# The first block's preparation in an attention and SwiGLU block: work moved from GpSimd to VectorE, loads and memsets reordered

## Chip, cores and metric

The kernel runs on one core of a Trainium2 chip. The metric is device time in microseconds (us); less is better. Engines: TensorE (PE in the profile; PEld is its weight load) multiplies, VectorE (DVE), ScalarE (ACT) and GpSimd (POOL) work on tiles, SyncE (SP) issues the transfers (DMAs) of one queue. Each engine works through its own instructions in the order in which the program gives them.

## The reference

A transformer block over x of 2048 positions by 512 features, all in float32: a modulation of six rows from the vector c, a layer norm with scale and shift, attention of 32 heads of 16 features over a sliding window of 256 positions, and a SwiGLU of 1792 features.

```python
mod = (silu(c) @ w_mod).reshape(1, 6, 1, 512)      # sa, ca, ga, sb, cb, gb
h = layernorm(x) * (1 + ca) + sa
x = x + ga * attention(h, wqkv, wo)                # causal, window 256, 32 heads
h = layernorm(x) * (1 + cb) + sb
x = x + gb * ((silu(h @ w1) * (h @ w3)) @ w2)
```

## The kernel before

The positions are cut into four blocks of 512 (`NB`), a block into four tiles of 128. A product in nearly full float32 is made of three products of float32r parts: a matrix is split into its rounded form (part 0) and the remainder (part 1), and part 0 by part 0, part 0 by part 1 and part 1 by part 0 are added up. So whatever TensorE multiplies has first to be cast and then subtracted.

The change lies in the opening, the first 100 us or so. There the order of all work is written out by hand: each step is handed to `at` with a time (in units of its own, none of the chip's), and all steps are recorded sorted by these times. What a step waits for follows from the data and from the buffers; the times only set each engine's order. The dictionary `W` and the dictionary `Y` hold them. `h0` is -40, the time of the first block.

What the opening does, with the names used below:

- `load_x` loads a tile of x into `xt` (six buffers, `XB`); `load_mod` loads four 256 KB pieces of w_mod into `stage`, `load_wv` (n=0) the four pieces of the values' weights into the same memory, `load_wqk` (n=0) a group's query and key weights into `wqr`. SyncE's queue issues all but c and the first modulation's pieces, which ScalarE's queue issues.
- `modulation(j, s)`: TensorE multiplies silu(c) with row block j of w_mod (`row`, L570 of the profile), ScalarE copies the result (`out`, L575), TensorE turns it into columns (`turn`, L583) and VectorE stores them in `modc` (L592). For j=2 and 5 it is instead spread by a product (L580), copied (L589) and stored to memory (`g_dr`, L590). The order of j is 0, 1, then 3, 4, 2, 5 among the values' products; the rows of 3 and 5 are the third and the sixth.
- `ln1(b)`: VectorE takes the statistics of four tiles (L335, L336), GpSimd the reciprocal root (L330), VectorE normalises (L340), TensorE transposes (L628) a feature group k of 128, ScalarE scales and shifts it (`h`, L347), VectorE makes part 0 (cast, L349) and part 1 (subtraction, L350) in `hT`.
- `load_wv` with n=1 makes part 0 of the values' weights for group k on ScalarE (`wvh`, L606), with n=2 part 1 on GpSimd (`wvl`, L608). `load_wqk` does the same for queries and keys: part 0 on ScalarE (L418), part 1 on GpSimd (L421).
- `values(t)`: twelve products (L650), three for each k, and a copy by ScalarE (L654). `unit_a(u)`: twelve products (`pj`, L433) for a head group and a block, three copies on ScalarE, two subtractions on GpSimd (`mix`, L451), and six transfers (`rows`, L456), two for each of three parts (qk0, qk1, qk2), into `ring`, the tile of keys and queries. `unit_b(u)`: the score products over `ring` (L486), which need all six, and their row maxima on VectorE (L493).
- `ring_fill(b)` writes the constant rows of `ring` for a block: five memsets of 1024 elements. For b=0 two are VectorE's, the rest GpSimd's.
- Three small tiles are made on VectorE behind the first block's statistics: `odd` (L305), `identr` (L398), the masks `later` and `mskr` (L393, L395). The masks are cut from `mskw`, which lies in the buffer of `wqr`, so the first load of wqk waits for them, and SyncE's queue behind it.

Each transfer counts up one of eight semaphores, in turn, and waits for the transfer eight before it.

Of the kernel before, what the change touches and what calls it, by code (L numbers as in the profile page):

```python
# [18 lines left out]
P = 128  # L19
KC = D // P  # L20
NT = S // P
NB = 4
BT = S // NB
# [13 lines left out]
         o=(9.93, 10.63), job=(-0.855, 2.493, 10.058))  # L37
# [6 lines left out]
W = dict(m=0.15, s=0.1, a=0.32, t=0.541, p=0.377, vs=1.762, vo=0.422, wq=-2.02, ws=-0.376, wv0=-1.811, wv=0.3, wvk=0.474, h0=0.539, h=6, hb=6.874, ls=3.287, la=1.146, rf=7.313, v=2, vt=1.75, m0=1.5, mt=0.7, ml=0.241, A=1.268, At=7.876, B=9.889)  # L44
MXB = 3
STB = 3
MODL = 'CECECECE'
NL = 3
XB = 6
PTB = 9  # L50
NU = NQ * NB
NP = NF // 2
# [236 lines left out]
def block_kernel(ctx: ExitStack, tc: tile.TileContext, x, wqk, wv, wo, w13, w2, c, wmod, out):  # L289
    nc = tc.nc  # L290
# [4 lines left out]
    ident = cst.tile([P, P], F32, name="ident")  # L295
# [4 lines left out]
    nc.gpsimd.memset(o32, 1.0 / 32)  # L300
    odd = cst.tile([P, 1], F32, name="odd")

    for hh in range(2):
        r = slice(64 * hh, 64 * hh + 64)
        nc.vector.tensor_reduce(  # L305
            out=odd[r], in_=ident[r].rearrange("p (c o) -> p c o", o=4)[:, :, 2 - 2 * hh:4 - 2 * hh],
            op=ALU.add, axis=mybir.AxisListType.XY)
    modc = cst.tile([P, 4, KC], F32, name="modc")
    sc32 = cst.tile([P, KC, 32], F32, name="sc32")

# [57 lines left out]
    ring = ap.tile([P, 3, 2, S], F32R, name="ring")  # L368
# [24 lines left out]
    nc.vector.tensor_scalar(later, mskk[:, 0], 0.0, None, op0=ALU.is_lt)  # L393
    mskr = ap.tile([P, 2, P], F32R, name="mskr")
    nc.vector.tensor_copy(mskr, mskk)  # L395
    mskk = mskr.bitcast(F32)
    identr = ap.tile([P, P], F32R, name="identr")
    nc.vector.tensor_copy(identr, ident)  # L398

    def ring_fill(b):  # L400
        for hh in range(2):
            k = ring.bitcast(F32)[:, 2 - 2 * hh, :, b * BT:(b + 1) * BT]
            eng = nc.vector if b == 0 and hh == 0 else nc.gpsimd
            eng.memset(k[:NM] if hh == 0 else k[:NS], 0.0)
            if hh:
                eng.memset(k[NS:NM], 1.0)
            eng.memset(k[NS:NS + 2], 1.0 - hh)

    WQ = {}

    def load_wqk(g, n):
        if n == 0:
            raw = a1.tile([P, KC, P], F32, name="wqr", bufs=1)
            nc.sync.dma_start(raw, wqk[g])
            WQ[g] = [None, None, raw]
        elif n == 1:
            WQ[g][0] = a1.tile([P, KC, P], F32R, name=f"wq0{g % 2}", bufs=1)
            nc.scalar.activation(WQ[g][0], WQ[g][2], AF.Copy)  # L418
        else:
            WQ[g][1] = a1.tile([P, KC, P], F32R, name=f"wq1{g % 2}", bufs=1)  # L420
            nc.gpsimd.tensor_tensor(out=WQ[g][1], in0=WQ[g][2], in1=WQ[g][0].bitcast(F32),  # L421
                                    op=ALU.subtract)

    def unit_a(u, t0, at, y=X):

# [130 lines left out]
    nc.vector.tensor_copy(sc32, sc[:, :, None].to_broadcast([P, KC, 32]))  # L556

    def modulation(j, s, t0, at):

        v = {}  # L560

        def bank(n):
            v[n] = psA.tile([P, BT], F32, name="mx", bufs=MXB)
            return v[n]

        def row():

            ps = bank(0)
            for k in range(KC):
                nc.tensor.matmul(ps[32 * k:32 * k + 32, :], sc32[:, k], stage[:, s, k], start=True,  # L570
                                 stop=True)

        def out():
            v["e"] = p0.tile([P, D], F32, name="h32", bufs=3)
            nc.scalar.activation(v["e"], v[0], AF.Copy)  # L575

        def turn():
            ps = bank(1)
            if j in (2, 5):
                nc.tensor.matmul(ps[:32], o32[:, :32], v["e"], start=True, stop=True)  # L580
                return
            for n in range(KC):
                nc.tensor.matmul(ps[:, n:n + 1], v["e"][:, n * P:(n + 1) * P], o32[:, 0:1],  # L583
                                 start=True, stop=True)

        def end():
            if j in (2, 5):
                r = p0.tile([P, D], F32, name="h32", bufs=3)
                nc.scalar.activation(r[:1], v[1][:1], AF.Copy)  # L589
                nc.sync.dma_start(g_dr[j // 5:j // 5 + 1, :], r[:1, :])  # L590
            else:
                nc.vector.tensor_scalar_add(modc[:, (0, 1, 0, 2, 3)[j]], v[1][:, :KC],  # L592
                                            float(j in (1, 4)))

        for n, fn in enumerate((row, out, turn, end)):
            at(t0 + W["m"] * n, fn)

# [3 lines left out]
    def load_wv(k, n):  # L601
        raw = stage[:, 0, k]
        if n == 0:
            nc.sync.dma_start(raw, wv[:, k])
        elif n == 1:
            nc.scalar.activation(wvh[:, k], raw, AF.Copy)  # L606
        else:
            nc.gpsimd.tensor_tensor(out=wvl[:, k], in0=raw, in1=wvh.bitcast(F32)[:, k],  # L608
                                    op=ALU.subtract)

    def ln1(b, ts, ta, th, at):
        v = {}
# [20 lines left out]
        for i in range(4):  # L633
            at(ts + W["s"] * i, lambda i=i: stats(i))
            at(ta + W["a"] * i, lambda i=i: apply(i))
            at(th + W["t"] * i, lambda i=i: turn(i))
            at(th + W["t"] * i + W["p"], lambda i=i: parts(i))
            if b + 1 < NB:
                at(th + (W["t"] * 3 + 0.1 if i > 1 else -0.5), lambda i=i: load_x(4 * b + 4 + i))
        at(ts + W["s"] * 3 + 0.1, rstd)  # L640

    def values(t, t0, at):
# [947 lines left out]
```

## Time and profile before

| | us |
|---|---|
| time, median of 3 runs (lowest to highest) | 989.64 (989.48 to 990.66) |
| profiled execution: its time | 987.77 |
| profiled execution: span of the page | 986.0 |
| third modulation's row on TensorE starts | 29.77 |
| sixth modulation's row on TensorE starts | 45.10 |
| first score product starts | 50.66 |

The last three come from the timeline of the profiled execution, counted from the span's start. Rows of a timeline give start and duration in us, the engine, the line, the operation, what it writes and reads, a count, and in brackets the idle time before it with what ended it. An engine's name with a q is its queue: there an instruction that only waits or issues.

### The profile page before, as it was taken

Reading aid. Unit: us, or ns where it says so; the run is one execution under the profiler, and the core shown is the slowest. Engines: PE = TensorE matmul, PEld = TensorE weight load, DVE = VectorE, ACT = ScalarE, POOL = GpSimd, SP = SyncE. Lnnn points to the kernel's source line nnn. Section 1 sums busy time; section 2 is a strip of 40 time slices with the busy share of each in tenths; the row PEclk is TensorE's granted clock in tenths of the full one; section 3 lists DMA queues with packets and bytes.
Section 4 is the critical chain, followed back from the end, with each engine's and each line's share of the span. In section 5 each row is a group of like instructions: output and inputs, shape, how many; then the busy total and the mean of one; then the engine's idle time right before and its main releaser. Section 6 shows DMA issues by size and latency. Waiting matters only on the chain.

```text
span 986.0 us, 17173 instructions
## 1 busy us (share of the span) xinstructions
PE 944.6 (96%) x5316; PEld 717.4 (73%) x5316; DVE 717.9 (73%) x1999; ACT 554.2 (56%) x1252; POOL 609.8 (62%) x775
## 2 busy tenths in 40 slices
PE   5999999999999999997888999999999999999998
PEld 2578777777777776764566778878888888888886
DVE  7775889899989999996467676755568655555455
ACT  3433887787878787874577864333445344433330
POOL 7441787787868686864476588897737555443420
PEclk9999999999999999997999999999999999999999
DMA  8621354444544444435891558765336423312102
GB/s 280 189 87 34 125 187 142 142 141 142 177 150 148 145 150 143 142 131 152 218 268 68 175 169 285 235 206 192 121 96 208 147 73 96 96 59 81 38 22 85
DMA packets 80671, 141.64 MB, mean 144 GB/s; under 512 B 9538, under 2 KB 22338, under 8 KB 80580
## 3 DMA queue, kind: packets, MB, share of 16 engines
q1 hardware_dynamic: 79860, 139.50, 43.8%
q10 hardware_dynamic: 720, 1.05, 0.3%
q8 instruction: 42, 0.69, 0.3%
q14 instruction: 49, 0.40, 0.1%
HBM read 85.72 MB, written 34.61 MB: 122 GB/s over the span
## 4 chain that ended last, share of the span: by engine, by line
PE 74%; POOL 8%; DVE 7%; DMA 6%; issue 2%; ACT 2%; SPq 1%; POOLq 0%; DVEq 0%; ACTq 0%
PE mx L1361 11%; PE st L1361 11%; PE mx L486 8%; PE pj L433 7%; PE st L736 7%; PE st L1454 6%; PE po L712 6%; PE mx L1454 6%; PE pj L1361 4%; PE st L650 3%; PE pj L1454 2%; POOL w L953 2%; POOL pt L764 2%; POOL qk L451 1%; DMA ring<-qk 1%
## 5 line engine op out<-in xcount | busy, mean ns | idle before, releaser
L493 DVE CUSTOM_DVE_ANT_0 junk<-mx,mskq 128x384 bf16<-128x384 f32 (+2 forms) x512 | 256.5, 527 | 35.4 <-PE mx L486 34.1
L953 POOL TENSOR_TENSOR w<-w,w 128x512 fp32r<-128x512 f32 (+2 forms) x56 | 107.7, 1936 | 124.4 <-ACT w L952 93.4
L486 PE MATMUL mx<-ring 96*128 96x384 f32 (+2 forms) x512 | 155.9, 342 | 9.9 <-DMA ring<-qk 6.9
L736 PE MATMUL st<-ring 100*128 100x384 f32 (+2 forms) x512 | 156.3, 346 | 2.8 <-ACT pt L748 1.4
L764 POOL TENSOR_SCALAR_AFFINE_SELECT pt<-pt 128x256 f32<-128x256 f32 x268 | 108.6, 408 | 73.4 <-ACT pt L757 63.1
L433 PE MATMUL pj<-hT,wq 128*128 128x512 f32 x384 | 136.3, 405 | 1.5 <-DVE hT L350 1.2
L486 PEld LDWEIGHTS mx<-ring 96*128 96x128 f32 x512 | 94.1, 190 | 43.5 <-DVE mt L493 25.0
L757 ACT ACTIVATE pt<-st 128x256 f32<-128x256 f32 x268 | 96.1, 386 | 41.9 <-DVE st L754 34.4
L736 PEld LDWEIGHTS st<-ring 100*128 100x128 f32 x512 | 95.8, 190 | 24.8 <-issue 8.0
L712 PE MATMUL po<-pt,vS 128*17 128x384 f32 (+2 forms) x1408 | 96.6, 391 | 1.4 <-POOL pt L764 0.9
L451 POOL TENSOR_TENSOR qk<-qkr,qk 128x512 fp32r<-128x512 f32 x64 | 82.7, 1292 | 15.9 <-ACT qkr L439 15.6
L754 DVE COPY_PREDICATED st<-later,st 128x128 f32<-128x128 uint8 x268 | 72.1, 291 | 10.2 <-PE st L736 6.3
L433 PEld LDWEIGHTS pj<-hT,wq 128*128 128x128 f32 x384 | 71.7, 190 | 8.7 <-DVE hT L350 1.5
L1432 ACT ACTIVATE wq<-g 128x512 fp32r<-128x512 f32 x28 | 17.7, 633 | 91.0 <-PE st L1454 31.6
L712 PEld LDWEIGHTS po<-pt,vS 128*17 128x17 f32 x1408 | 33.2, 97 | 47.2 <-issue 21.3
L1392 DVE TENSOR_TENSOR t<-mx,t 128x512 f32<-128x512 f32 x50 | 34.4, 688 | 45.4 <-PE mx L1361 31.0
L1361 PE MATMUL st<-b,w 128*128 128x512 f32 x258 | 64.6, 392 | 0.8 <-DVE b L1258 0.4
L1361 PE MATMUL mx<-b,w 128*128 128x512 f32 x252 | 62.7, 394 | 1.1 <-ACT mx L976 1.1
L748 ACT ACTIVATE pt<-st 128x384 f32<-128x384 f32 (+2 forms) x128 | 52.7, 434 | 17.5 <-DVE st L744 13.9
L1392 DVE TENSOR_TENSOR t<-st,t 128x512 f32<-128x512 f32 x47 | 32.3, 687 | 41.5 <-PE st L1361 23.8
L781 POOL TENSOR_SCALAR_AFFINE_SELECT sm<-sm 128x256 f32<-128x256 f32 x109 | 41.9, 407 | 28.1 <-ACT sm L771 24.1
L1361 PEld LDWEIGHTS st<-b,w 128*128 128x128 f32 x258 | 48.1, 188 | 11.9 <-DVE b L1258 0.8
(265 smaller groups left out, 2088.8 us busy)
## 6 DMA issues: line engine op xcount, KB each, us to landing
ring<-qk SPq DMA_DIRECT2D x192, 128.0 KB
o_dr<-os SPq DMA_DIRECT2D x32, 256.0 KB
w<-wsum SPq DMA_DIRECT2D x14, 512.0 KB
w<-w2g SPq DMA_DIRECT2D x14, 512.0 KB
jb<-in_w SPq DMA_DIRECT2D x24, 256.0 KB
wraw<-in_w SPq DMA_DIRECT2D x7, 768.0 KB
w<-wraw SPq DMA_DIRECT2D x14, 384.0 KB
vS<-in_wmod SPq DMA_DIRECT2D x20, 256.0 KB
```

What stands on the lines that cost most here:

```text
L433: nc.tensor.matmul(v["ps"], WQ[g][w][:, n // 3], hTp(i, n // 3, b * BT, BT), start=(n == 0), stop=(n == 3 * KC - 1))
L451: nc.gpsimd.tensor_tensor(out=v[n], in0=v["raw"], in1=v[1].bitcast(F32), op=ALU.subtract)
L486: nc.tensor.matmul(v[i][:, :n], queries(NS, a, gq, 1), keys(NS, hh, a, k0, gq + 1 - k0), start=True, stop=True)
L493: nc.vector.tensor_tensor_reduce(out=junk[:, :n], in0=v[i][:, :n], in1=mskq[:, 3 * P - n:], scale=1.0, scalar=-3e38, op0=ALU.add, op1=ALU. ...
L712: nc.tensor.matmul(po[32 * i:32 * i + DH + 1, qb * P:(qb + nq) * P], vS[:, kb, 4 * g + i], pts[i // 2][:, i % 2, c0:c0 + nq], start=first, ...
L736: nc.tensor.matmul(ps[:, :nq], keys(NM, hh, a, kb, 1), queries(NM, a, kb, nq), start=True, stop=not plus)
L754: nc.vector.copy_predicated(ps[:, 0], later, ps[:, 2])
L757: nc.scalar.activation(held[u, j, a][:, hh, :2], v[j, a, hh][:, :2], AF.Exp, scale=SCALE)
L764: nc.gpsimd.affine_select(out=pt[:, :, 2 * m], in_=pt[:, :, 0], **w)
L953: sch.op(eng, lambda: on_eng(eng).tensor_tensor(out=lo(), in0=src(), in1=hi().bitcast(F32), op=ALU.subtract), 0.06 + 0.0024 * n if eng == ...
L1361: nc.tensor.matmul(ps(bk), WT[s, n][w][:, col], BB[t, k][r], start=start and c == 0, stop=stop and c == 5, skip_group_check=True)
L1454: nc.tensor.matmul(ps(bk), tiles[hk + (h,)][:, i * P:(i + 1) * P], w2_of(last, y, f), start=(m == 0), stop=(m == 5))
```

## The change

It concerns the opening alone.

- VectorE's small tiles move: the masks (`fill_masks`) come ahead of everything, silu(c)'s copy (`fill_sc`), `odd` and `identr` (`fill_odd`) between the second and the third tile's statistics.
- `ring_fill` takes one half at a time and is GpSimd's altogether. Both halves for block 0 and the first half for block 1 (seven memsets) come ahead of the first reciprocal root; the second half for block 1 (three) is placed at r1=1.55.
- SyncE's queue has the values' four pieces ahead of wqk, then x for block 1. All four tiles of a later block are loaded behind that block's predecessor's transposes, in four buffers instead of six. The pieces for j=3, 4, 2, 5 follow each other.
- All four wvh are ScalarE's before the first h. Of the wvl GpSimd makes two (`wp`), VectorE two, ahead of the first cast. Part 1 of the first wqk is VectorE's, behind the first block's parts.
- A modulation's copy out is split into two of 256 columns.
- Unit 0 starts at A0=2.6 instead of 1.268: its products stand further back among those of the values. Ahead of the third modulation's row TensorE has 24 products, where it had 27; the other three come between the fourth and the sixth.
- On SyncE the six transfers of unit 0 stood as qk0, qk1, store of the first `g_dr`, x, qk2, store of the second `g_dr`, wqk. Now: first store, x (four tiles), qk0, qk1, second store, wqk, qk2.

```diff
-W = dict(..., wq=-2.02, ws=-0.376, wv0=-1.811, wv=0.3, wvk=0.474, h0=0.539, ..., ml=0.241, A=1.268, ...)
+W = dict(..., wq=(-1.8, 1.0, 1.5), wv0=-1.811, wvh=(-0.7, -0.65, -0.6, -0.55), wvl=(-0.5, -0.45, -0.3, -0.25), wp=2, r1=1.55, A0=2.6, h0=0.539, ..., ml=1.3, A=1.268, ...)
-XB = 6
+XB = 4
...
-    for hh in range(2):
-        ...
+    def fill_odd():
+        for hh in range(2):
+            ...
+        nc.vector.tensor_copy(identr, ident)
...
+    def fill_masks():
+        nc.vector.tensor_copy(mskr, mskw[:, :2])
+        nc.vector.tensor_scalar(later, mskw[:, 0], 0.0, None, op0=ALU.is_lt)
...
-    def ring_fill(b):
-        for hh in range(2):
-            k = ring.bitcast(F32)[:, 2 - 2 * hh, :, b * BT:(b + 1) * BT]
-            eng = nc.vector if b == 0 and hh == 0 else nc.gpsimd
-            eng.memset(k[:NM] if hh == 0 else k[:NS], 0.0)
-            if hh:
-                eng.memset(k[NS:NM], 1.0)
-            eng.memset(k[NS:NS + 2], 1.0 - hh)
+    def ring_fill(b, hh):
+        k = ring.bitcast(F32)[:, 2 - 2 * hh, :, b * BT:(b + 1) * BT]
+        nc.gpsimd.memset(k[:NM] if hh == 0 else k[:NS], 0.0)
+        if hh:
+            nc.gpsimd.memset(k[NS:NM], 1.0)
+        nc.gpsimd.memset(k[NS:NS + 2], 1.0 - hh)
...
-            nc.gpsimd.tensor_tensor(out=WQ[g][1], in0=WQ[g][2], in1=WQ[g][0].bitcast(F32),
-                                    op=ALU.subtract)
+            eng = nc.gpsimd if g else nc.vector
+            eng.tensor_tensor(out=WQ[g][1], in0=WQ[g][2], in1=WQ[g][0].bitcast(F32), op=ALU.subtract)
...
-            nc.scalar.activation(v["e"], v[0], AF.Copy)
+            for n in range(2):
+                nc.scalar.activation(v["e"][:, n * 256:n * 256 + 256], v[0][:, n * 256:n * 256 + 256], AF.Copy)
...
-            nc.gpsimd.tensor_tensor(out=wvl[:, k], in0=raw, in1=wvh.bitcast(F32)[:, k],
-                                    op=ALU.subtract)
+            eng = nc.gpsimd if k < W["wp"] else nc.vector
+            eng.tensor_tensor(out=wvl[:, k], in0=raw, in1=wvh.bitcast(F32)[:, k], op=ALU.subtract)
...
-                at(th + (W["t"] * 3 + 0.1 if i > 1 else -0.5), lambda i=i: load_x(4 * b + 4 + i))
+                at(th + W["t"] * 3 + 0.1, lambda i=i: load_x(4 * b + 4 + i))
...
-    ring_fill(0)
     h0 = -40.0
+    at(h0 - 9, fill_masks)
+    for n in range(2):
+        at(h0 - 9 + 0.1 * n, lambda n=n: ring_fill(0, n))
+    at(h0 - 8.7, lambda: ring_fill(1, 0))
+    at(h0 - 3 + 1.5 * W["s"], fill_sc)
+    at(h0 - 3 + 1.6 * W["s"], fill_odd)
...
     for n in range(3):
-        at(h0 + (W["wq"] if n == 0 else W["ws"] + n * 0.02), lambda n=n: load_wqk(0, n))
+        at(h0 + W["wq"][n], lambda n=n: load_wqk(0, n))
     for k in range(KC):
-        for n in range(3):
-            at(h0 + (W["wv0"] if n == 0 else W["wv"] + 0.02 * n) + W["wvk"] * k * (n > 0),
-               lambda k=k, n=n: load_wv(k, n))
+        at(h0 + W["wv0"], lambda k=k: load_wv(k, 0))
+        at(h0 + W["wvh"][k], lambda k=k: load_wv(k, 1))
+        at(h0 + W["wvl"][k], lambda k=k: load_wv(k, 2))
...
-        at(h - W["rf"], lambda b=b: ring_fill(b))
+        for n in range(2):
+            if b > 1 or n:
+                at(h - W["rf"] if b > 1 else h0 + W["r1"], lambda b=b, n=n: ring_fill(b, n))
...
-        unit_a(u, h0 + W["A"] + W["At"] * u, at, Y)
+        unit_a(u, h0 + (W["A"] + W["At"] * u if u else W["A0"]), at, Y)
```

More of the change, by code (lines that the diff above doesn't have):

```diff
@@ L43 @@
 MODE = 'CDCPCCCP'
-W = dict(m=0.15, s=0.1, a=0.32, t=0.541, p=0.377, vs=1.762, vo=0.422, wq=-2.02, ws=-0.376, wv0=-1.811, wv=0.3, wvk=0.474, h0=0.539, h=6, hb=6.874, ls=3.287, la=1.146, rf=7.313, v=2, vt=1.75, m0=1.5, mt=0.7, ml=0.241, A=1.268, At=7.876, B=9.889)
+W = dict(m=0.15, s=0.1, a=0.32, t=0.541, p=0.377, vs=1.762, vo=0.422, wq=(-1.8, 1.0, 1.5), wv0=-1.811, wvh=(-0.7, -0.65, -0.6, -0.55), wvl=(-0.5, -0.45, -0.3, -0.25), wp=2, r1=1.55, A0=2.6, h0=0.539, h=6, hb=6.874, ls=3.287, la=1.146, rf=7.313, v=2, vt=1.75, m0=1.5, mt=0.7, ml=1.3, A=1.268, At=7.876, B=9.889)
 MXB = 3
@@ L301, in block_kernel @@
     odd = cst.tile([P, 1], F32, name="odd")
-    for hh in range(2):
[L304 to L307, printed above, removed]
+    def fill_odd():
+        for hh in range(2):
+            r = slice(64 * hh, 64 * hh + 64)
+            nc.vector.tensor_reduce(
+                out=odd[r], in_=ident[r].rearrange("p (c o) -> p c o", o=4)[:, :, 2 - 2 * hh:4 - 2 * hh],
+                op=ALU.add, axis=mybir.AxisListType.XY)
+        nc.vector.tensor_copy(identr, ident)
     modc = cst.tile([P, 4, KC], F32, name="modc")
@@ L392, in block_kernel @@
     later = ap.tile([P, P], mybir.dt.uint8, name="later")
-    nc.vector.tensor_scalar(later, mskk[:, 0], 0.0, None, op0=ALU.is_lt)
     mskr = ap.tile([P, 2, P], F32R, name="mskr")
-    nc.vector.tensor_copy(mskr, mskk)
+    identr = ap.tile([P, P], F32R, name="identr")
+    def fill_masks():
+        nc.vector.tensor_copy(mskr, mskw[:, :2])
+        nc.vector.tensor_scalar(later, mskw[:, 0], 0.0, None, op0=ALU.is_lt)
     mskk = mskr.bitcast(F32)
-    identr = ap.tile([P, P], F32R, name="identr")
-    nc.vector.tensor_copy(identr, ident)
-    def ring_fill(b):
-        for hh in range(2):
-            k = ring.bitcast(F32)[:, 2 - 2 * hh, :, b * BT:(b + 1) * BT]
-            eng = nc.vector if b == 0 and hh == 0 else nc.gpsimd
-            eng.memset(k[:NM] if hh == 0 else k[:NS], 0.0)
-            if hh:
-                eng.memset(k[NS:NM], 1.0)
-            eng.memset(k[NS:NS + 2], 1.0 - hh)
+    def ring_fill(b, hh):
[4 more added lines that the diff above has]
+        nc.gpsimd.memset(k[NS:NS + 2], 1.0 - hh)
     WQ = {}
@@ L555, in block_kernel, with fill_sc @@
     nc.scalar.activation(sc, c_sb, AF.Silu)
-    nc.vector.tensor_copy(sc32, sc[:, :, None].to_broadcast([P, KC, 32]))
+    def fill_sc():
+        nc.vector.tensor_copy(sc32, sc[:, :, None].to_broadcast([P, KC, 32]))
     def modulation(j, s, t0, at):
```

## The prediction

> **What bounds the kernel now.** I read the page first, then the timeline of the first 60 us, then windows of stages, then the queues.
>
> ```profile
> span 986.0 us, 17173 instructions
> PE 944.6 (96%) x5316; PEld 717.4 (73%) x5316; DVE 717.9 (73%) x1999; ACT 554.2 (56%) x1252; POOL 609.8 (62%) x775
> PE 74%; POOL 8%; DVE 7%; DMA 6%; issue 2%; ACT 2%; SPq 1%; POOLq 0%; DVEq 0%; ACTq 0%
> ```
>
> TensorE is busy for 96% of the span and holds 74% of the chain of waits. From the first score product on, TensorE and VectorE have the same instructions in the same order in both programs, so a shift of TensorE there should reach the end one for one. The stages before it decide (columns of a window: TensorE busy, its weight loads, VectorE, ScalarE, GpSimd, granted clock, DMA share, GB/s):
>
> ```profile
> 17.16:20.57 3.41, 1.91 (x10) 1.08 (x9) 3.12 (x3) 3.41 (x7) 3.33 (x3) 1.00 0.98 339
> 20.57:23.98 3.41, 3.41 (x10) 2.17 (x8) 3.38 (x3) 0.90 (x2) 3.41 (x3) 0.50 1.02 372
> 23.98:27.40 3.42, 2.18 (x9) 1.16 (x8) 3.35 (x5) 0.00 (x0) 1.74 (x2) 1.00 0.75 272
> 29.77:45.10 15.33, 15.21 (x89) 9.04 (x88) 10.74 (x16) 7.90 (x13) 9.05 (x8) 1.00 0.69 207
> 45.10:50.66 5.56, 5.38 (x25) 2.76 (x24) 4.17 (x11) 1.78 (x3) 1.89 (x3) 1.00 0.52 159
> ```
>
> From 17 to 27 us TensorE is starved, and for 3.41 us its clock is halved. From 29.77 on it is full. 29.77 and 45.10 are the starts of the third and the sixth modulation product (L570), 50.66 that of the first score product (L486). In the starved stretch VectorE sets the pace:
>
> ```profile
> 16.61 0.78 ACT L347 ACTIVATE h<-st,modc 128x512 f32<-128x512 f32 x1 [1.29 <-PE st L628]
> 17.29 0.62 ACT L606 ACTIVATE wvh<-vS 128x512 fp32r<-128x512 f32 x1
> 17.42 0.95 DVE L349 CAST hT<-h 128x512 fp32r<-128x512 f32 x1 [1.17 <-ACT h L347]
> 17.81 0.77 ACT L347 ACTIVATE h<-st,modc 128x512 f32<-128x512 f32 x1
> 18.40 1.64 DVE L350 TENSOR_TENSOR hT<-h,hT 128x512 fp32r<-128x512 f32 x1
> 19.46 6.26 POOL L608 TENSOR_TENSOR wvl<-vS,wvh 128x512 fp32r<-128x512 f32 x4
> 26.19 0.41 DVE L349 CAST hT<-h 128x512 fp32r<-128x512 f32 x1
> 26.32 0.50 PE L650 MATMUL st<-wvh,hT 128*128 128x512 f32 x1 [0.89 <-DVE hT L350]
> 26.63 0.69 DVE L350 TENSOR_TENSOR hT<-h,hT 128x512 fp32r<-128x512 f32 x1
> 27.24 0.69 DVE L335 BATCH_NORM_STATS2 bst<-xt 128x6 f32<-128x512 f32 x1
> ```
>
> A cast takes 0.41 us and a subtraction 0.69 once GpSimd is idle (26.19 on), but 0.95 and 1.64 beside its work: the two take turns. TensorE last waits for these parts at 26.32.
>
> **The change part by part.** *Masks before the queue.* SP stood 3.0 us on the cast of the masks, since the first wqk load reuses their scratch:
>
> ```profile
> SPq L414 <- DVE mskr L395: 3.0, 1, 3.0
> SPq L546 <- DMA vS<-in_wv: 2.3, 2, 2.1
> 19.28 2.33 SPq L546 DMA_DIRECT2D vS<-in_wmod  x4
> 5.50:11.00 5.50, 2.35 (x8) 0.55 (x10) 3.58 (x13) 0.23 (x2) 0.54 (x1) 1.00 1.05 397
> 11.00:12.50 1.50, 1.50 (x8) 0.36 (x4) 1.20 (x3) 0.00 (x0) 1.44 (x3) 1.00 0.40 119
> 14.00:18.00 4.00, 4.00 (x33) 3.48 (x32) 2.66 (x5) 2.51 (x5) 3.87 (x4) 1.00 0.82 200
> ```
>
> Before, the DMA engines fall from 397 to 119 GB/s at 11 us for want of issues, and the last two value blocks land only about 19.2 and 19.9 us (SP waits 2.1 and 0.2 us for them before it goes on at 19.28). Now the four loads (1.05 MB) follow the modulation loads and begin near 11, where the rate falls. At 397 GB/s they take 2.6 us, at the 200 GB/s of 14 to 18 us 5.3, so they are in between 14 and 17 us. I take the early end, since the queue no longer runs dry there; as late as before is a rival.
>
> *Key rows written early.* Seven GpSimd memsets now stand ahead of the reciprocal root (L330).
>
> ```profile
> 3.30 0.95 POOL L404 MEMSET ring<- 96x1024 f32 x1
> 10.46 1.03 POOL L330 TENSOR_TENSOR rs0r<-rs0v,nhalf 128x4 f32<-128x4 f32 x1 [5.21 <-DVE rs0v L328]
> 14.21 0.60 ACT L575 ACTIVATE h<-mx 128x512 f32<-128x512 f32 x1 [0.91 <-PE mx L570]
> 15.19 0.16 DVE L592 TENSOR_SCALAR modc<-mx 128x4 f32<-128x4 f32 x1 [0.17 <-PE mx L583]
> ```
>
> Seven of 0.95 with some 0.05 between them, from 3.30 on, end at 10.3, just before the root. If VectorE's copies delay them, by 0.7 us at the most (four copies), the normalised rows still end before the modulation column at 15.19, which they used to meet anyway: zero. If they slowed the first loads, all would slip; the 3.30 memsets lie beside the first loads already and show no price that I can separate, so 0 to 0.5.
>
> *First block.* ScalarE's copy out is split (0.70 a pair against 0.60, an estimate: 0.2 fixed in an activation of 4 columns, which leaves 0.4 for 256). Then it makes all four wvh before any h. Starts are 0.52 apart behind a wvh and 0.68 behind an h (rows at 16.61, 17.29, 17.81): wvh at 14.8, 15.3, 15.8, 16.4, h at 16.9, 17.6, 18.2, then wq and the last h at 19.5. GpSimd's first wvl runs 15.5 to 16.8; VectorE's first ends near 17.4; its second takes turns with GpSimd's second (1.6) and ends near 19.0. The first cast meets a memset that was not moved far enough (r1=1.55 puts three behind wvl): 0.95 instead of 0.41, so 19.9; its subtraction 20.6. Three more pairs at 1.05 (26.19 to 27.24) and two brushes with memsets (0.1 each) give 24.0, and the wq part (0.6), now VectorE's too, 24.6. So GpSimd is not idle, as said, for the first half of it.
>
> On TensorE 12 products are then done or waiting, the 13th needs that wq part. So 13th at 24.7, and 12 products reach the third modulation at 27.5 instead of 29.77 (in the timeline 14 such products fill 26.32 to 29.77, 3.45 us with a slow first one; I take 2.8 for 12). Three products went behind it (0.7). The sixth modulation: 27.5 + 15.33 + 0.7 = 43.5, against 45.10: **1.6 us gained**. The halved clock of 20.57 to 23.98 stays (TensorE hardly works in the window before it), and hides in the waits. The loads of block 1 and of modulation 3 wait for the last transposes (18.5) now, XB being 4; with 2.8 us from issue to landing (between the waits worked out next) and 0.7 for each of seven more of 256 KB at 372 GB/s the last block that modulation 3 needs is in at 26.2, 1.3 us before it is used.
>
> *What stands behind g_dr on SP.* This is where I expect the gain to go. Row parts of unit 0 were issued by 46.1:
>
> ```profile
> 44.88 1.20 SPq L456 DMA_DIRECT2D ring<-qk  x2
> 48.70 0.25 SPq L590 DMA_DIRECT2D g_dr<-h  x1
> 49.00 0.34 SPq L414 DMA_DIRECT2D wqr<-in_wqk  x1
> 106.55 5.02 SPq L456 DMA_DIRECT2D ring<-qk  x6
> 113.53 0.41 PE L486 MATMUL mx<-ring 96*128 96x384 f32 x1 [0.17 <-DMA ring<-qk]
> 444.57 5.86 SPq L456 DMA_DIRECT2D ring<-qk  x6
> 452.81 0.66 PE L486 MATMUL mx<-ring 96*128 96x384 f32 x1 [5.87 <-DMA ring<-qk]
> 371.12 3.90 DMA ring<-qk
> ```
>
> With unit 0 at A0=2.6 its last part (qk2) is issued behind the second g_dr store and the next wqk load. That store waits for the sixth modulation's two copies and product, 48.70 - 45.10 = 3.6 us after its start, 3.7 with split copies. So store 47.2, load 47.5, the two parts 47.9 to 49.1. Scores that waited for such parts began 1.96 us after the last issue ended (113.53) and 2.38 after it (452.81); in a third place the landing took 3.90 from the issue. I take 2.2, one load more in front than in the first case: the first score at 51.3. TensorE would come to it at 43.5 + 5.56 = 49.1. So it stands still for 2.2 us (2.0 to 3.5), everything behind it on TensorE too, the value products with it, and the first score is 0.65 (0.7 below) *later* than 50.66.
>
> *Clock.* Windows of 3.41 us from 17.16:
>
> ```profile
> 532.57:535.98 3.41, 2.03 (x9) 1.39 (x8) 3.38 (x3) 2.17 (x4) 3.41 (x3) 1.00 0.01 2
> 535.98:539.39 3.41, 3.39 (x15) 2.45 (x15) 3.38 (x5) 2.77 (x5) 1.84 (x3) 1.00 0.03 7
> 546.22:549.63 3.41, 1.82 (x6) 0.97 (x7) 3.34 (x10) 1.88 (x4) 0.00 (x0) 1.00 0.93 318
> 549.63:553.05 3.42, 3.42 (x10) 2.65 (x9) 2.63 (x11) 3.30 (x9) 0.94 (x1) 0.50 1.04 363
> ```
>
> With 1.82 or 1.91 us busy in a window the next ran at half clock, with 2.03 or 2.18 it did not. A stall of 2.2 us leaves under 1.95 in some window wherever the grid falls, except where its edge cuts the stall in the middle. TensorE is full behind it, so half of 3.41 us is lost: 1.7.
>
> The Trainium skill, TensorE: Matmul & The Clock Gate, section "HAM oscillation — how this bites in real kernels", gives the rule "no PE-idle gaps >~3.4µs". By that rule a stall of 2.2 us costs no clock, and the sum would stop at 0.7 us; the windows at 17.16 and 546.22, each more than half busy, speak against it.
>
> Sum on the profiled execution: 987.77 (span 986.0 and 1.77 around it) + 0.7 + 1.7 = 990.2. The median of runs lies 1.87 above that execution, so 989.64 + 2.4 = **992.0**. With landing and load bounds (1.96 to 3.4, memsets 0 to 0.5) its own range is 990.6 to 993.8.
>
> **The rivals.**
> *Stall without the slow window* (its edge cuts the stall, or the clock tolerates it): 989.64 + 0.7 = 990.3. For it: 2.03 us busy were enough once. Against: two thirds of a window would be idle.
> *The gain survives.* If the first products keep full clock (from 20.57 on, 1.7 us saved) because the faster parts fill the window before, the sixth modulation comes at 41.8, the first score at 49.7, 1.0 earlier than 50.66; with no slow window behind it 988.6, not slower. It decides at TensorE being busy for over 1.95 us in the window that ends at 20.57. Against it: the first cast ends only at 19.9.
> *Value weights still late*, about 19.9 as before: the first h then starts at 20.4, the cast ends 21.7, the wq part 26.2, the sixth modulation is at 45.1, the first score at 52.9: 2.3 + 1.7, so 993.6. For it: 200 GB/s in 14 to 18 us, which no row explains. Against: the loads are issued some 3 us earlier.
>
> **How the numbers follow.** Slow window and stall 0.46, stall alone 0.24, gain survives 0.12, weights late 0.18. About 0.2% (2.0 us: under 987.7 or over 991.6) is what a measurement can tell here. The first case lies two thirds above 991.6, the fourth wholly, the second hardly: slower 0.50. Half of the third with luck of the clock's grid: faster 0.08. Range of all cases: 988.4 to 994.4.
>
> **What would show it.** Right: casts and subtractions near 0.41 and 0.69 from 20 us on; no SP wait on the mask cast; third modulation near 27.5, sixth near 43.5; the first score waiting over 2 us for ring<-qk, starting near 51.3; a window of clock 0.50 behind it. Wrong: a first score before 50.0 or no DMA wait there; a wvh waiting for its load beyond 17; or TensorE's order points after 55 us shifted by another amount than the end of the kernel.

## The result, and the profile after

The changed kernel takes 995.12 us in the median of 7 runs (992.73 to 999.64), the kernel before 989.48 beside it (987.88 to 990.66): by the medians it is 5.6 us slower. The ratio taken from all runs is 1.0061, 95% interval 1.0040 to 1.0082. The forecast was 2.4 us slower, with a range to 994.4. The profiled execution of the changed kernel took 994.10, its span is 992.4, against 987.77 and 986.0 before.

The page of the changed kernel, as the rows shown of before: the engines' busy time and the chain of waits by engine. TensorE has 1.8 us more to do by the record (its products last longer at half clock), and in the chain DMA has 9% where it had 6%.

```profile
span 992.4 us, 17173 instructions
PE 946.4 (95%) x5316; PEld 718.4 (72%) x5316; DVE 715.2 (72%) x2000; ACT 554.0 (56%) x1258; POOL 607.3 (61%) x774
PE 69%; POOL 10%; DMA 9%; DVE 5%; issue 3%; ACT 3%; SPq 1%; POOLq 0%; DVEq 0%; ACTq 0%
```

The opening went nearly as worked out. From the timeline of the changed kernel (start, duration, engine, line, what it writes and reads):

```profile
14.68 2.19 ACT L613 ACTIVATE wvh<-vS 128x512 fp32r<-128x512 f32 x4
19.02 0.70 DVE L353 CAST hT<-h 128x512 fp32r<-128x512 f32 x1
22.72 0.42 DVE L353 CAST hT<-h 128x512 fp32r<-128x512 f32 x1
23.79 0.68 DVE L426 TENSOR_TENSOR wq<-wqr,wq 128x512 fp32r<-128x512 f32 x1
27.69 1.50 PE L576 MATMUL mx<-vS,sc 128*32 128x512 f32 x8
43.99 1.06 PE L576 MATMUL mx<-vS,sc 128*32 128x512 f32 x8
53.34 0.45 PE L490 MATMUL mx<-ring 96*128 96x128 f32 x1 [3.57 <-DMA ring<-qk]
```

All four wvh run without a break from 14.68, so their loads were there. The wq part ends at 24.47 (24.6 was forecast), the third modulation starts at 27.69 (27.5; 29.77 before), the sixth at 43.99 (43.5; 45.10 before). At the sixth modulation 1.1 us are gained. Then TensorE stands for 3.57 us, and the first score product starts at 53.34, 2.7 later than before. SyncE's queue and the chain of waits of the changed kernel show what it stood for:

```profile
42.86 1.77 SPq L542 DMA_DIRECT2D xt<-in_x  x4
44.72 2.69 SPq L460 DMA_DIRECT2D ring<-qk  x4
47.66 0.24 SPq L597 DMA_DIRECT2D g_dr<-h  x1
47.96 0.35 SPq L418 DMA_DIRECT2D wqr<-in_wqk  x1
48.55 1.53 SPq L460 DMA_DIRECT2D ring<-qk  x2
...
44.26 5.27 DMA xt<-in_x
...
49.54 3.57 DMA ring<-qk
...
53.34 0.45 PE mx L490
```

A row of the chain is start, length and what held the work up. A tile of x, issued at 44.26, took 5.27 us to land, and only then could the second of the last two row transfers be issued (a transfer waits for the one eight before it; SyncE waited 0.6 us in all for tiles of x here). That one landed 3.57 later, at 53.11. Windows of 3.41 us of the changed kernel (columns as in the prediction: length, TensorE, its loads, VectorE, ScalarE, GpSimd, clock, DMA share, GB/s):

```profile
18.10:21.51 3.41, 1.78 (x7) 0.97 (x6) 3.34 (x5) 2.07 (x4) 3.30 (x4) 1.00 0.69 238
21.51:24.92 3.41, 3.41 (x9) 2.27 (x8) 3.34 (x7) 0.00 (x0) 0.28 (x1) 0.50 0.80 220
43.99:49.77 5.78, 5.54 (x24) 2.58 (x23) 4.84 (x9) 1.90 (x5) 2.40 (x3) 1.00 0.91 280
48.82:52.23 3.41, 0.94 (x5) 0.42 (x3) 1.62 (x5) 0.00 (x0) 1.49 (x2) 1.00 0.67 186
52.23:55.64 3.41, 2.30 (x6) 1.95 (x7) 0.30 (x2) 0.00 (x0) 3.28 (x4) 0.50 0.01 3
55.64:59.06 3.42, 3.42 (x10) 2.74 (x10) 1.06 (x5) 0.60 (x1) 0.95 (x1) 0.50 0.00 0
```

The DMA engines are busy for 91% of the stretch that leads to the wait. The window that holds the wait has TensorE at 0.94 us, and not one but two windows at half clock follow: in the first TensorE was busy for 2.30 of 3.41 us, and that did not bring the clock back. So 2.30 and 3.42 us run at half speed, which costs half of each, 2.9 us. A score product that both programs have in the same place behind, one that waits for VectorE, starts at 72.44 before and here 5.45 later:

```profile
72.44 0.44 PE L486 MATMUL mx<-ring 96*128 96x384 f32 x1 [1.01 <-DVE mt L493]
...
77.89 0.45 PE L490 MATMUL mx<-ring 96*128 96x384 f32 x1 [1.02 <-DVE mt L497]
```

Of these 5.45, 2.68 are there at the first score product. The other 2.77 arise in the stretch with the two windows at half clock, whose price worked out above is 2.9. This product is called the mark below. At the end of the span the shift is 6.4, so not all of it is made in the opening; the last section shows where another trace lost more.

### The profile page after: what moved, and what is told of

Same layout as the page of the kernel before. It is cut to its first block, busy times and chain, and to the rows that moved or that the text cites. A ratio compares the mean times of both kernels' runs of the same rounds, so it can differ in the third digit from the quotient of the medians.

```text
span 992.4 us, 17173 instructions
## 1 busy us (share of the span) xinstructions
PE 946.4 (95%) x5316; PEld 718.4 (72%) x5316; DVE 715.2 (72%) x2000; ACT 554.0 (56%) x1258; POOL 607.3 (61%) x774
## 4 chain that ended last, share of the span: by engine, by line
PE 69%; POOL 10%; DMA 9%; DVE 5%; issue 3%; ACT 3%; SPq 1%; POOLq 0%; DVEq 0%; ACTq 0%
PE st L1376 9%; PE mx L1376 8%; PE mx L490 8%; PE pj L437 8%; PE st L751 7%; PE po L727 6%; PE st L1469 5%; PE mx L1469 5%; PE st L657 4%; PE pj L1376 3%; PE pj L1469 2%; POOL w L968 2%; POOL e L877 2%; POOL pt L779 2%; PE mx L1114 1%
## 5 line engine op out<-in xcount | busy, mean ns | idle before, releaser
L490 PE MATMUL mx<-ring 96*128 96x384 f32 (+2 forms) x512 | 156.3, 343 | 16.3 <-DMA ring<-qk 12.2
```

Source lines behind the costliest of these rows:

```text
L490: nc.tensor.matmul(v[i][:, :n], queries(NS, a, gq, 1), keys(NS, hh, a, k0, gq + 1 - k0), start=True, stop=True)
```

## The experiments

Eleven kernels ran, in three sets, each on one chip. The kernel before ran in each: its medians there were 991.19, 989.65 and 989.71, so only ratios to the kernel before of the same set are compared. The ratios are taken from all runs and are not quotients of the medians. A single profile is one draw of where the clock's windows fall; the ratio comes from all runs. All in one table (times from the timeline of each profile; in brackets after the first score product what it waited for its rows; "half" counts the windows at half clock between 48 and 62 us):

| kernel | third mod. | sixth mod. | first score | half | mark | ratio to before, 95% |
|---|---|---|---|---|---|---|
| before | 29.77 | 45.10 | 50.66 (0) | 0 | 72.44 | |
| changed | 27.69 | 43.99 | 53.34 (3.57) | 2 | 77.89 | 1.0061, 1.0040 to 1.0082 |
| after_again | 26.76 | 42.45 | 52.64 (4.41) | 2 | 77.33 | 1.0045, 1.0030 to 1.0059 |
| fill_stall | 27.00 | 42.86 | 51.98 (filled) | 0 | 74.35 | 1.0005, 0.9991 to 1.0019 |
| before_a0 | 30.46 | 46.52 | 54.68 (2.45) | 1 | 78.16 | 1.0037, 1.0020 to 1.0055 |
| a0_back | 31.46 | 46.45 | 52.49 (0.27) | 0 | 74.34 | 1.0018, 1.0003 to 1.0033 |
| qk2_first | 26.83 | 42.52 | 50.98 (2.69) | 1 | 74.46 | 1.0029, 1.0010 to 1.0047 |
| xb6 | 27.17 | 42.87 | 50.88 (2.25) | 1 | 74.30 | 1.0014, 0.9999 to 1.0030 |
| wp4 | 29.63 | 45.33 | 54.40 (3.29) | 1 | 77.88 | 1.0038, 1.0024 to 1.0052 |
| rows_early | 26.95 | 43.69 | 49.31 (0) | 0 | 72.62 | 0.9996, 0.9982 to 1.0009 |
| rows_xb6 | 26.83 | 43.04 | 48.66 (0) | 0 | 70.44 | 0.9985, 0.9973 to 0.9996 |
| rows_xb6_warm | 26.91 | 43.11 | 48.73 (0) | 0 | 70.51 | 0.9981, 0.9971 to 0.9991 |
| rows_xb6_wp4 | 28.72 | 44.93 | 50.54 (0) | 0 | 72.43 | 0.9999, 0.9988 to 1.0010 |

The theory after the result (A): the opening gains, unit 0's last row part comes too late, and the clock falls behind that wait. The rival (B): the moved preparation itself costs the time.

**before_a0.** The kernel before with one edit of the change alone.

```diff
-        unit_a(u, h0 + W["A"] + W["At"] * u, at, Y)
+        unit_a(u, h0 + (W["A"] + W["At"] * u if u else 2.6), at, Y)
```

> The kernel before with unit 0 started at 2.6 instead of 1.268, nothing else. Theory A: the sixth modulation stays near 45.1 and the store near 48.7, the last row part is issued near 51, the first score product waits 2.3 to 3.5 for it from 50.7 on, one or two half-clock windows follow, and the median is 993.5 to 995.5, so this one edit would be slower than before by as much as the whole change. Rival B: 989 to 990, no wait at the first score product.

The wait is there and the loss too, a ratio of 1.0037, without any of the moved preparation. The timeline of this kernel, the queue and TensorE:

```profile
46.52 1.06 PE L570 MATMUL mx<-vS,sc 128*32 128x512 f32 x8
50.12 0.25 SPq L590 DMA_DIRECT2D g_dr<-h  x1
...
50.87 1.21 SPq L456 DMA_DIRECT2D ring<-qk  x2
54.68 0.30 PE L486 MATMUL mx<-ring 96*128 96x128 f32 x1 [2.45 <-issue]
```

The store stands 3.6 behind the sixth modulation's start, as in the kernel before, and the rows behind the store. The row of the first score product names no releaser for its 2.45; asked who waited for the transfers of L456, the profile gives this product, with 2.5 us. The sixth modulation came 1.4 later than expected. Two windows of the opening (21.4 to 28.2) ran at half clock here and one in the trace of before; whether that is the whole reason was not tested. So 1.4 of the 5.7 at the mark belong to the opening of this trace. The rival (989 to 990, no wait) is out.

**fill_stall.** The changed kernel with 15 products that nothing reads ahead of the first score product.

```diff
+    def keep(n):
+        if n == 0:
+            jb0["ps"] = psA.tile([P, BT], F32, name="mx", bufs=MXB)
+        nc.tensor.matmul(jb0["ps"], hTp(0, 0, 0, P), wvh[:, 0], start=True, stop=True)
+    for n in range(15):
+        at(h0 + W["B"] - 0.001, lambda n=n: keep(n))
```

> The changed kernel with 15 idle products of 512 columns (their result is read by nothing) on TensorE right ahead of the first score product, about 3.5 us of work at full clock, so that TensorE is busy through its wait. Theory C (half of the loss is the clock, which a mostly idle window halves): the first score product starts at 53.3 as before, no half-clock window follows, and the end comes 2.7 earlier: median near 992.4. Rival D (the windows at half clock only stand beside the loss; or the clock falls for another reason): the first score at 53.3, clock 0.50 from 52.2 on all the same, median near 995.

Timeline and windows of this kernel:

```profile
48.48 3.66 PE L716 MATMUL mx<-wvh,hT 128*128 128x512 f32 x15
51.98 0.22 PE L490 MATMUL mx<-ring 96*128 96x128 f32 x1
...
50.40:53.81 3.41, 3.41 (x17) 2.80 (x16) 0.60 (x4) 0.00 (x0) 3.22 (x4) 1.00 0.03 7
```

The first score product comes 9.1 behind the sixth modulation, about as in the changed kernel (9.35), and at 51.98 instead of 53.3 mostly because the sixth modulation was early too (42.86). The clock stays full. From the first score product to the mark it takes 22.4 us here, 24.6 in the changed kernel and 21.8 before, so 2.2 of the 2.77 are gone; theory C gave 2.7. The ratio, 1.0005 against 1.0061 and 1.0045, falls by more than that, and part of it is the first score product, which came 1.4 earlier. So the half clock is a cost of its own that follows from the idle time. The extra products end just where the score starts, so when the rows alone would have let it start isn't seen.

**qk2_first** and **xb6** take one of two suspected causes of the late rows away each: the place behind the store, and the four tiles of x in front.

```diff
# qk2_first
-            at(t0 + y["row"][r], lambda r=r: rows(r), "qk_rows")
+            at(t0 + (5.53 if u == 0 and r == 2 else y["row"][r]), lambda r=r: rows(r), "qk_rows")
# xb6
-XB = 4
+XB = 6
-                at(th + W["t"] * 3 + 0.1, lambda i=i: load_x(4 * b + 4 + i))
+                at(th + (W["t"] * 3 + 0.1 if i > 1 else -0.5), lambda i=i: load_x(4 * b + 4 + i))
```

> The changed kernel with the last row part of unit 0 alone moved ahead of the second store of g_dr and the wqk load. Theory A1 (what delays it is its place behind the store, which waits for the sixth modulation): its issue ends near 48.7 instead of 50.1, the first score product starts at 50.7 to 51.7 instead of 53.34, and the median is 990 to 992.5. Rival A2 (the four tiles of x and the rows issued from 42.9 on fill the transfer engines, so the place on the queue matters little): only the 256 KB of wqk are out of the way, 0.7 to 0.9, the first score product starts at 52.4 or later, and the median is 993.5 to 994.5.

> The changed kernel with x in six buffers again and the first two tiles of each later block loaded ahead of the transposes, as in the kernel before; the row parts stay behind the second store. Rival A2 of the earlier run (the four tiles of x fill the transfer engines ahead of the rows): 512 KB less stand in front, so the last part lands 1.2 to 1.6 sooner behind the sixth modulation's start than in the changed kernel (7.7 to 8.1 instead of 9.35 from that start to the first score product), and the median is 1.5 to 3 below the changed kernel's: ratio to the kernel before 1.002 to 1.004. Theory A1 (the place behind the store decides): the distance stays above 9.0, ratio 1.004 to 1.007.

The chain of waits of qk2_first, and then of xb6:

```profile
46.64 4.26 DMA ring<-qk
...
50.98 0.30 PE mx L490
```

```profile
46.53 0.25 SPq L597
...
47.28 2.92 DMA ring<-qk
...
50.88 0.45 PE mx L490
```

In qk2_first the last transfer is issued at 46.64, ahead of the store, and its issue ends at 47.23, 1.5 sooner than expected; yet it takes 4.26 us to land, behind four tiles of x. In xb6 the rows stand behind the store, but the one issued at 47.28 lands in 2.92. From the sixth modulation to the first score it is 8.5 and 8.0 us, against 9.35 and 10.2 in the two traces of the changed kernel. Neither edit alone removes the wait (2.69 and 2.25 are left), and in these traces one window at half clock follows instead of two. The ratio of xb6, 1.0014, lies below its expectation (1.002 to 1.004) and can't be told from 1. So both theories hold a part: the place on the queue and the transfers in front.

The time from the end of the last issue to the first score product sorts the traces by what was issued ahead. It is 3.26, 3.07 and 2.86 us with four tiles of x ahead and the store between (changed, after_again, wp4), 2.39 and 2.60 with two tiles (xb6, before_a0), and 3.75 and 4.10 where the rows follow the four tiles directly (qk2_first, and a0_back below).

**a0_back.** The changed kernel with unit 0 where it was.

```diff
-A0=2.6
+A0=1.268
```

> The changed kernel with A0 back at 1.268 and nothing else different. Theory A (the loss is the wait of the first score product for unit 0's last row parts, which stand behind the second store of g_dr, and the clock that it costs): 27 products stand ahead of the third modulation again, it starts near 28.4, the sixth near 44.0; the last part of unit 0 is issued ahead of the second store; the first score product starts between 49.4 and 50.2 with a wait under 0.6, no half-clock window behind it, and the median is near 988.3 (987.5 to 989.5). Rival B (the moved preparation itself costs the time, by more work on VectorE and another phase of the clock): the median stays at 993 or more, whatever A0 is.

The wait shrinks to 0.27, no half clock follows, and still the ratio is 1.0018, where under 1 was expected. The opening was misjudged: the third and the sixth modulation come at 31.46 and 46.45, where 28.4 and 44.0 were expected. Timeline and windows of its opening:

```profile
23.71 0.80 PE L437 MATMUL pj<-hT,wq 128*128 128x512 f32 x1 [3.28 <-DVE wq L426]
...
21.22:24.63 3.41, 0.92 (x2) 0.82 (x3) 3.31 (x8) 0.00 (x0) 0.00 (x0) 0.50 0.95 301
24.63:28.05 3.42, 3.42 (x9) 2.65 (x9) 2.30 (x7) 0.00 (x0) 0.84 (x1) 0.50 0.95 356
```

With unit 0's products further forward, one that needs the wq part stands among TensorE's first, and VectorE now makes that part behind everything else: TensorE waits 3.28, and two windows there run at half clock. The late start of unit 0 hangs together with the move of the wq part. Undone alone, it takes the loss at the scores away and puts another into the opening: the sixth modulation is 1.35 later than before, the mark 1.9.

**wp4.** The changed kernel with all four wvl on GpSimd.

```diff
-wp=2
+wp=4
```

> The changed kernel with all four wvl on GpSimd (two of them are VectorE's in the change). It tells what VectorE's share brings in the opening. Theory F (taking turns with GpSimd sets the pace of the casts and subtractions): GpSimd's work lasts to about 24.7 instead of 21.8, casts take 0.95 and subtractions 1.6 until then, the wq part ends near 26.5 instead of 24.5, the third modulation starts near 29.0 to 29.5 instead of 27.7, and the kernel is 1.3 to 2 slower than the changed one: ratio 1.007 to 1.009. Rival G (two subtractions less on VectorE make up for it): third modulation within 0.5 of 27.7, ratio 1.005 to 1.0065.

The opening is 1.9 slower in this trace, as theory F said (29.63 against 27.69, with two windows at half clock in it against one), but the ratio, 1.0038, is not above the changed kernel's (1.007 to 1.009 was expected). The mark is at the same place (77.88 and 77.89): the wait was 3.29 instead of 3.57 and fell almost whole into the window from 51.61 to 55.03, and one window at half clock followed instead of two. Behind a wait that costs more than the gain, the gain can't be read; the test was repeated below without that wait.

**rows_early** and **rows_xb6.** Unit 0's copies, subtractions and transfers right behind its products, and then x in six buffers too (the edit of xb6).

```diff
+        if u == 0:
+            y = dict(y, ev=(4.35, 4.25, 4.3), mix=(4.4, 4.45), row=(4.5, 4.55, 4.6))
         for n in range(3):
             at(t0 + y["ev"][n], lambda n=n: out(n), "out")
```

> The changed kernel with unit 0's three copies, two subtractions and six row transfers placed directly behind its products, ahead of the first store of g_dr and of the tiles of x; A0 stays at 2.6. Theory A: TensorE's opening stays as in the changed kernel (third modulation 26.8 to 27.7, sixth 42.5 to 44.0, by the phase of the clock), the last part is issued before 45 and lands before 47.5, the first score product follows the products ahead of it with no wait (5.5 to 5.8 behind the sixth modulation's start, so 48.0 to 49.8 against 50.66), no window of half clock follows, and the kernel is faster than the kernel before by 1 to 3 us in the median (ratio 0.997 to 0.999). Rival B (the moved preparation costs time elsewhere): the wait is gone, but the ratio to the kernel before stays above 1.001. Rival E (the copies of unit 0, ahead of others on ScalarE, delay the second block's parts): TensorE stops for these between the fourth modulation and the first score, by 0.5 or more.

The rows are in time, the first score product starts 1.35 ahead of before without a wait, and the loss of the change is gone. But the ratio of 0.9996 falls short of the 0.997 to 0.999 expected, and the mark is at 72.62, not ahead of before. Where it was lost, from the timeline of rows_early:

```profile
44.95 1.78 SPq L544 DMA_DIRECT2D xt<-in_x  x4
50.08 0.69 DVE L339 BATCH_NORM_STATS2 bst<-xt 128x6 f32<-128x512 f32 x1 [0.79 <-DMA xt<-in_x]
57.85 0.33 PE L637 MATMUL st<-ident,xt 128*128 128x128 f32 x1 [0.84 <-DVE xt L344]
```

Four tiles of x behind the first store are late for VectorE's statistics, and the third block's transposes then wait 0.84 for the normalised rows. Rival E, other parts late on ScalarE, holds a little: TensorE waits 0.45 and 0.24 for the copies of the two modulations that are spread, and from the third modulation to the sixth it takes 16.7 instead of 16.3. rows_xb6 asks whether the tiles are it:

> rows_early with six buffers of x and the first two tiles of a block loaded ahead of the transposes. Theory A: rows_early started its first score product 1.35 us ahead of the kernel before and lost it again where the third block's transposes waited 0.84 for its normalised rows, late since all four tiles of x came behind the first store. Here the statistics of these tiles end before 50, no wait over 0.3 stands at the transposes near 57, the first score product starts at 48.0 to 49.5, and the kernel is faster than the kernel before by 1 to 2.5: ratio 0.9975 to 0.999. Rival B: same as rows_early, 0.9995 to 1.001, since VectorE is the bound there.

```profile
37.53 6.14 SPq L460 DMA_DIRECT2D ring<-qk  x6
48.66 0.22 PE L492 MATMUL mx<-ring 96*128 96x128 f32 x1
70.44 0.44 PE L492 MATMUL mx<-ring 96*128 96x384 f32 x1 [1.02 <-DVE mt L499]
```

They are: six transfers issued between 37.53 and 43.67, the first score product at 48.66 without a wait, the mark 2.0 ahead of before. With a ratio of 0.9985 (0.9973 to 0.9996) this kernel beats both, 988.03 beside 989.71; the gain is small, and the interval ends close to 1.

**rows_xb6_warm** and **rows_xb6_wp4** take rows_xb6 apart: six products that nothing reads between the last transposes and the first value product, and wp=4.

```diff
# rows_xb6_warm
+    def keep(n):
+        if n == 0:
+            xt["keep"] = psA.tile([P, BT], F32, name="mx", bufs=MXB)
+        nc.tensor.matmul(xt["keep"], wvh[:, 0, :P], wvh[:, 0], start=True, stop=True)
+    for n in range(6):
+        at(h0 - W["h0"] + W["t"] * 3 + 0.001, lambda n=n: keep(n))
# rows_xb6_wp4
-wp=2
+wp=4
```

> rows_xb6 with six idle products of 512 columns on TensorE (1.4 us at full clock, their result is read by nothing) between the last transposes of the first block and its first value product, where TensorE waits 1.6 us. Theory C: no window between 17 and 27 us is granted half clock, the third modulation starts at 26.8 or before in this trace whatever the phase, and the median is 0 to 0.8 below rows_xb6. Rival: VectorE's parts pace these products anyway; no difference that can be told.

> rows_xb6 with all four wvl on GpSimd. Theory F (VectorE's share brings most of the opening's gain): the third modulation starts 1.5 to 2.5 later than in rows_xb6 and the end comes as much later: ratio to the kernel before 1.000 to 1.001. Rival G: the earlier loads bring it, and the ratio is that of rows_xb6 within 0.0005.

The first leaves no half clock in the opening from 11 us on, but the third modulation is at 26.91 against 26.83: VectorE paces the opening, and 0.9981 can't be told from 0.9985. The second, from its timeline:

```profile
18.58 1.65 DVE L354 TENSOR_TENSOR hT<-h,hT 128x512 fp32r<-128x512 f32 x1
20.15 1.49 DVE L353 CAST hT<-h 128x512 fp32r<-128x512 f32 x1
```

A subtraction takes 1.65 again and a cast 1.49, beside GpSimd's work; the third modulation is 1.9 later than in rows_xb6 (28.72), the mark 2.0 later, the ratio 0.9999 and the median 989.64 against 988.03. So the gain of the opening goes with VectorE's two wvl. Loads and memsets in their new order bring nothing by themselves that these runs can tell; they were not taken out one by one.

**after_again.** The changed kernel itself in the last set.

> The changed kernel itself once more, beside runs of the kernel before on this chip. Theory A: the distance from the sixth modulation's start to the first score product is again 9.2 to 9.5, with a wait of 3.4 to 3.7, whatever the start of the sixth modulation is; ratio to the kernel before 1.004 to 1.006. Rival H (the first result was a bad draw of the clock's phase): ratio under 1.003 with the same wait.

From its timeline and its SyncE waits (us, times, longest):

```profile
47.91 1.66 SPq L460 DMA_DIRECT2D ring<-qk  x2
52.64 0.45 PE L490 MATMUL mx<-ring 96*128 96x128 f32 x1 [4.41 <-DMA ring<-qk]
...
SPq L460 <- DMA xt<-in_x: 1.6, 2, 1.1
```

The loss is no bad draw. But the distance I expected (9.2 to 9.5) was wrong: it is 10.2. The opening was 1.5 faster here, and the rows landed only 0.7 sooner: SyncE was ready sooner, but waited 1.1 for a tile of x to land before it could issue the rows. In this trace the first score product is bound by the transfers in front and not by the sixth modulation, so the faster opening only made the wait longer.

## Why the prediction was wrong in size and right in place

- *The opening*: right. Parts, wq part, third and sixth modulation came within 0.5 of the working in this trace (in after_again the two modulations were 0.7 and 1.1 ahead of it), and the sixth 1.1 ahead of before where 1.6 was forecast. That VectorE's share brings it stands on wp4 and rows_xb6_wp4 (the third modulation 1.9 later in each).
- *The mechanism of the loss*: right. The last row part of unit 0 stands behind the second store and the wqk load, TensorE stands for it, and the clock falls behind (before_a0, fill_stall).
- *The step that failed* is "I take 2.2" for the time from the last issue to the first score product. It measured 3.26 (issued by 50.08, score at 53.34). The issues themselves ended at 50.08 instead of 49.1: half of that is the sixth modulation (43.99 instead of 43.5), the rest mostly SyncE's wait for tiles of x, a term that stood at nothing. So of the 2.0 by which the first score missed 51.3, 1.1 are the landing, 0.5 the issues and 0.5 the sixth modulation.
- *What stands in its place*: I took the landing from two places further on (1.96 and 2.38) and only counted the commands ahead on the queue. How much is issued ahead, and how closely, was left out: four tiles of x, 1 MB, begin to be issued at 42.86, and from 43.99 on the engines are at 91% until TensorE gets there. The changed kernel loads all four in one go behind the transposes, and I had weighed that edit only for the second block. The same time is 2.39 in xb6, where two of the tiles are not ahead; the distance from the sixth modulation falls by 1.3 with it. The bytes alone are not the measure, since six loads of 256 KB stood ahead of the place that gave 2.38 as well. Worked out from the queue's rows and the sizes of the transfers, 2.25 MB were issued there within 9.3 us, 2.0 MB within 7.2 in the changed kernel, 1.5 within 6.8 in xb6 and 1.75 within 5.8 in qk2_first (3.75). So the time grows roughly with the rate of issue; what makes it so inside the engines stays open. The Trainium skill, DMA: Bandwidth & Descriptors, section "Latency and other measured facts", speaks of about 2 us of fixed cost for a transfer, less under lighter load; the 1.96 is near that, and the 2.8 to 4.6 from issue to landing in these kernels (some 0.6 of it the issue itself) lie above it.
- *The clock term* was mis-sized: 1.7 for one window, 2.77 for two. The wait reached into a second window, and 2.30 of 3.41 us busy in it were not enough to come back. Where one window followed it cost 1.7: in qk2_first the first score is 0.3 late and the mark 2.0. Which of the two comes depends on the length of the wait and on where the windows' edges fall (wp4: 3.29 us, one window), and the edges are luck.
- *The rule weighed against the trace* (no idle gaps above some 3.4 us; the Trainium skill, TensorE: Matmul & The Clock Gate, "HAM oscillation — how this bites in real kernels") would have spared waits of 2.25, 2.45 and 2.69 us: xb6, before_a0 and qk2_first each had a window at half clock behind it. So an idle gap shorter than a window is enough; the share of a window that TensorE is busy fits most windows, though not as a sharp limit (last section).
- *The sum*: 0.65 and 1.7 were forecast, 2.68 and 2.77 measured at the mark. On the medians 5.6 (4.2 in after_again) against 2.4. That a shift behind 55 us reaches the end one for one held only roughly: 5.45 at the mark and 6.4 at the end of the span here, 4.9 and 10.4 in after_again. A difference between the ends of two single traces is therefore no measure of the change; the ratio over all runs is.
- *The other rivals*: the value weights were not late. That the gain survives was ruled out as the changed kernel stands, but rows_xb6 shows it surviving once rows and tiles are in time.

## What to carry to other kernels

When work is moved so that a queue's issues come closer together, count the bytes that are issued ahead of the one that someone waits for, and in how short a time, and not only the commands: a landing time taken where the queue is issued loosely is no price for a dense stretch. An idle time of TensorE costs its own length; where it leaves a window of 3.41 us less than some 1.9 us busy, it mostly costs up to half of each window that follows too, until one that is nearly full. So read the windows behind the stall as well. And an early gain is only worth what the next fixed point leaves of it: look for what that point waits for before trusting the gain.

## What the runs showed of the hardware

The way back to full clock needs more than the way down. A window at half clock with TensorE busy for 2.30 us (changed kernel) or 2.62 (after_again, from 51.85) was followed by another at half clock, while 2.03 us were enough to keep the full clock in the kernel before. In the thirteen traces all windows at half clock with up to 2.94 us busy were followed by another (28 of them), and all with 3.03 or more by full clock (52). The two nearest are both in before_a0:

```profile
21.35:24.76 3.41, 2.94 (x7) 1.43 (x6) 3.38 (x3) 0.00 (x0) 3.41 (x3) 0.50 1.06 392
24.76:28.18 3.42, 3.42 (x8) 2.25 (x8) 3.35 (x6) 0.00 (x0) 0.69 (x1) 0.50 0.21 77
519.70:523.11 3.41, 3.03 (x9) 2.45 (x9) 2.73 (x2) 3.38 (x8) 3.41 (x3) 0.50 0.44 145
523.11:526.53 3.42, 3.42 (x17) 2.82 (x16) 3.42 (x6) 0.99 (x3) 2.52 (x2) 1.00 0.96 311
```

The way down has no such clean limit in these traces. Most windows under 1.9 us busy were followed by half clock, but not the one from 584.71 in the changed kernel, nor the one at the same place in ten other traces (1.62 to 1.74 us busy); and in the kernel before one with 2.91 us busy (from 440.41) was. What sets these apart stays open.

```profile
584.71:588.12 3.41, 1.63 (x10) 1.08 (x10) 2.68 (x3) 3.19 (x6) 3.17 (x6) 1.00 0.20 77
588.12:591.53 3.41, 3.41 (x18) 2.82 (x17) 1.33 (x2) 1.84 (x4) 2.56 (x4) 1.00 0.56 207
```

The windows do not start with the program: in the two traces of the changed kernel the half clock behind the scores' wait begins at 52.23 and at 51.85, which is not a whole number of windows apart. That the third modulation started at 27.69 in one and 26.76 in the other is not the clock's doing, though one had a window at half clock from 21.51 and the other none: at the first transposes, 15.83 against 15.07, most of the difference was there.

The spread between runs of one program is 7 us here (992.73 to 999.64). One source shows in after_again, whose profiled execution was the slowest of its runs: later on, TensorE waited for row transfers again.

```profile
191.40 0.42 PE L490 MATMUL mx<-ring 96*128 96x384 f32 x1 [1.37 <-DMA ring<-qk]
```

The window that holds this wait was busy for 1.92 us, the next ran at half clock, and the shift against the kernel before grew there from 5.5 to 8.2 us. Where the rest comes from stays open.
